# Attention's exponentials per head with a bias, and a later Square in the weight conversion

## The chip, the cores and the metric
One core of one Trainium2 chip runs the whole program in one launch. Its engines work side by side, each through its own queue in order: TensorE (PE for matmuls, PEld for the weight loads that go ahead of them), VectorE (DVE), ScalarE (ACT), GpSimd (POOL), and SyncE (SP), which only issues DMA transfers. The metric is the device time in microseconds (us) of one execution. Before the change it is 1010.89 us, the median of three runs (1010.03 to 1013.91).

## The reference
Three layers follow each other.

```python
k_p, v_p = mean of k, v over groups of 8 positions       # (4, 8, 72, 64)
scores = q @ k_p.T / 8                                   # (4, 8, 576, 72)
attn = exp(scores - max(scores)); attn /= attn.sum() + 1e-9
x = (attn @ v_p) as (2304, 512)
logits = x @ w_gate + log1p(exp(x @ w_noise)) * noise    # 8 experts
top2 = the two largest; weights = softmax over these two
out[token] = sum over its two experts e of weight * relu(x @ w1[e]) @ w2[e]
h = out @ w_in; g = max(0.01 * h, h); result = g @ w_out # 512 -> 2048 -> 512
```

All is float32, apart from `w_in` and `w_out`, which arrive as 64-bit floats and are narrowed to 32 bits on the chip.

## The kernel before
**Attention** goes over 18 tiles of 128 tokens. For one tile, `scores` multiplies the queries with the pooled keys of all 8 heads into one PSUM tile `qk` of two banks (8 heads of 72 columns, 576 in all). DVE reduces it to the maximum of each token and head (`mx`, 128x8, L364) and then subtracts that from all 576 columns into an SBUF tile `sm` (L366). `exponents` runs one exp over the 576 columns on ACT, with the scale 1/64 inside (L372). `transposed_exponents` transposes the result on PE in two halves of three (L380), and ACT copies each half out of PSUM (`at`, L381). `weighted` multiplies with the pooled values into another PSUM tile `av` (L388), ACT drains it (`avs`, L403), and `normalized` divides: DVE forms the reciprocal `rc` (L407, L408), POOL multiplies (L410, L413). `qk` and `av` take turns in three PSUM buffers.

The loop is skewed. In the turn of tile t, PE is given `scores(t+2)`, `transposed_exponents(t+1)` and `weighted(t)` in this order; its order is as written in the code. Those of DVE, ACT and POOL are made by a planner at compile time. Between these steps DVE also works on the router (`route`, with `work(budget)`), sums the keys of the next batch (`setup_keys`, L306) and splits the first expert weights (`split_half`, L156); POOL sums the values of the next batch (L324 to L326).

**The experts.** Each of 8 experts has up to 640 tokens. Float32 products are made of three matmuls on a high and a low part. For each expert, 8 calls of `hidden` (L742) are followed by 5 calls of `expert_out` (L763), each with a `transposed` (L215, L217, L218), which brings in a tile of the next expert's tokens. In `hidden`, ACT applies relu into the high part (L751), and DVE forms the low part (L752); the PSUM tile `ph` has two buffers. In `expert_out`, ACT copies the result out (`ys`, L773), and that PSUM tile has two buffers too. `feed` loads weights and splits them into two parts (ACT L154, DVE L156).

**The conversion** of the 64-bit weights is spread over the experts by calls of `narrow`. A call does a stage each for different pieces of 256 columns, of which there are 64: (1) for the 32 pieces of `w_in`, in pairs, a high and a low part of a converted tile (ACT L670, DVE L672); (2) the second half of the conversion of the last piece, a comparison and a product on DVE (L689), and sums on POOL (L700); (3) the first half of the conversion of another piece: four integer and float operations on DVE (L708, L711, L714, L715), then a sum on POOL (L718) and a Square on ACT (L719), which writes over a word that L715 has read; the comparison L689 of the next call reads it; (4) the load of a new piece. In this part of the kernel the orders of DVE and ACT are as written in the code, so what stands behind a waiting instruction waits too. PE's order here is the planner's.

A piece that is loaded in one call is first worked on two calls later, so 64 pieces need 69 calls until the last high and low parts are written. They are given so: 4 in the first expert's second pass of `hidden` and 3 behind it, 9 for each of the experts 1 to 6 (4 in `hidden`, at f = 0, 2, 4, 6, and 5 in `expert_out`), and 8 in the `hidden` of expert 7. That is 69.

**The last layer** (from 620 us on) gathers each token's two expert results and runs 512 to 2048 to 512 with the converted weights. The change leaves its code as it is.

Of the kernel before, what the change touches and what calls it, by code (L numbers as in the profile page):

```python
# [10 lines left out]
F32 = mybir.dt.float32  # L11
# [4 lines left out]
AF = mybir.ActivationFunctionType  # L16
ALU = mybir.AluOpType
# [4 lines left out]
P = 128  # L22
B, H, S, D = 4, 8, 576, 64
POOL = 8
J = S // POOL
# [3 lines left out]
E = 8  # L29
# [27 lines left out]
FH, FK, NF = 2, 2, 2  # L57
# [34 lines left out]
def pieces(t):  # L92
    got, n, end = [], t * P, (t + 1) * P
    while n < end:
        b = n // S
        m = min(end, (b + 1) * S) - n
        got.append((b, n - b * S, n - t * P, m))
        n += m
    return got
# [3 lines left out]
def body(ctx: ExitStack, tc, qT, kT, v, wgc, noise, eye, cst, w1, w2, win, wout, out):  # L103
    nc = tc.nc
# [53 lines left out]
    def feed(n, upto, pool=False):  # L158

        while loading:  # L160
            split_half(pool)
        for _ in range(n):
            if state["next"] < 2 * min(len(chunks), upto):
                c, h = divmod(state["next"], 2)
                state["next"] += 1
                raw = rawp.tile([P, 512], F32, tag="raw", name="raw")
                nc.sync.dma_start(raw, chunks[c][:, h * 512 : (h + 1) * 512])
                loading.append((c, h, raw))
# [33 lines left out]
    def gather(e, k):  # L202
        xg[e, k] = st.tile([P, DM], F32, tag="st", name="xg")
        i = k * E + e
        nc.gpsimd.indirect_dma_start(
            out=xg[e, k],
            out_offset=None,
            in_=x_d[0 : T1 * P if k < K1 else N, :],
            in_offset=bass.IndirectOffsetOnAxis(ap=gidx[:, i : i + 1], axis=0),
        )  # L210

    def transposed(src, dst, k):
        pt = b1.tile([P, 4, P], F32, tag="b1", name="xtp")
        for d in range(4):
            nc.tensor.transpose(pt[:, d, :], src[:, d * P : (d + 1) * P], ident)  # L215
        sl = slice(k * P, (k + 1) * P)
        nc.scalar.activation(dst[:, :, 0, sl], pt, AF.Copy)  # L217
        nc.vector.tensor_tensor(  # L218
            dst[:, :, 1, sl], pt, dst[:, :, 0, sl].bitcast(F32), op=ALU.subtract
        )  # L220

    with ExitStack() as actx:
        big = actx.enter_context(tc.tile_pool(name="qkav", bufs=3, space=PSUM))
        wk = actx.enter_context(tc.tile_pool(name="attw", bufs=2))
# [124 lines left out]
        sm, ex, at = {}, {}, {}  # L349

        def scores(t):
            ps = big.tile([P, 2, 512], F32, tag="big", name="qk")
            for b, s0, m0, m in pieces(t):
                for pr in range(4):
                    nc.tensor.matmul(
                        ps[m0 : m0 + m, pr // 2, (pr % 2) * 144 : (pr % 2) * 144 + 144],
                        qt[b][:, pr, s0 : s0 + m],
                        KB[b][:, pr, :],
                        start=True,
                        stop=True,  # L360
                    )
            view = ps[:, :, 0:288].rearrange("p a (h j) -> p a h j", j=J)
            mx = wk.tile([P, 2, 4], F32, tag="mx", name="mx")
            nc.vector.tensor_reduce(mx, view, axis=AX.X, op=ALU.max)  # L364
            sm[t] = wk.tile([P, 2, 4, J], F32, tag="sm", name="sm")
            nc.vector.tensor_tensor(  # L366
                sm[t], view, mx.unsqueeze(3).to_broadcast([P, 2, 4, J]), op=ALU.subtract
            )

        def exponents(t):  # L370
            ex[t] = sm[t].rearrange("p a h j -> p (a h j)")
            nc.scalar.activation(ex[t], ex[t], AF.Exp, scale=1.0 / 64.0)  # L372

        def transposed_exponents(t):
            at[t] = wk.tile([96, 6, P], F32, tag="at", name="at")
# [238 lines left out]
        for t in range(-2, T):  # L614
            if t + 2 < T:
                scores(t + 2)
# [11 lines left out]
            if t + 2 < T:  # L628
                exponents(t + 2)
# [32 lines left out]
    loaded, converting, parted = [], [], []  # L662

    def narrow():

        if parted and parted[0][1] is not None:
            i, part, w8, x = parted[0]
            sl = slice(512 * x, 512 * x + 512)
            hi = cv.tile([P, 512], F32R, tag="hi", name="cvhi", bufs=1)
            nc.scalar.activation(hi, w8[:, sl], AF.Copy)  # L670
            nc.sync.dma_start(combos[i][:, part, 0, sl], hi.bitcast(F32))
            nc.vector.tensor_tensor(  # L672
                w8[:, sl].bitcast(F32R), w8[:, sl], hi.bitcast(F32), op=ALU.subtract
            )
            nc.sync.dma_start(combos[i][:, part, 1, sl], w8[:, sl])
            parted[0][3] += 1
            if x:
                parted.pop(0)
        if converting:
            c, part, k, mf = converting.pop(0)  # L680
            if c < 8:
                w = cv.tile([P, CV], F32, tag="w", name="cvw")
            else:
                if part % 2 == 0:
                    w8 = cv.tile([P, 1024], F32, tag="cvq", name="cvq")
                    parted.append([c - 8, None, w8, 0])
                w8 = parted[-1][2]
                w = w8[:, part % 2 * CV : (part % 2 + 1) * CV]
            nc.vector.scalar_tensor_tensor(w, k, SMALL, mf, op0=ALU.is_ge, op1=ALU.mult)  # L689
            if c < 8:  # L690
                nc.sync.dma_start(singles[c][:, part * CV : (part + 1) * CV], w)
            elif part % 2:
                q = lambda i: w8[:, i * P : (i + 1) * P]
                for d, x, y, op in (
                    (S1, A21, A22, ALU.add),
                    (S2, S1, A11, ALU.subtract),
                    (S3, A11, A21, ALU.subtract),
                    (S4, A12, S2, ALU.subtract),
                ):
                    nc.gpsimd.tensor_tensor(q(d), q(x), q(y), op=op)  # L700
                parted[-1][1] = part // 2
        if len(loaded) > 1 or loaded and state["narrowed"] == 16 * 1024 // CV:
            c, part, raw = loaded.pop(0)
            low, high = raw[:, :, 0], raw[:, :, 1]
            a = cv.tile([P, CV], I32, tag="a", name="cva", bufs=1)
            m = cv.tile([P, CV], I32, tag="m", name="cvm")
            mf, hf, k = m.bitcast(F32), high.bitcast(F32), low.bitcast(F32)
            nc.vector.tensor_scalar(  # L708
                a, high, 3, 0x3FFFFFF8, op0=ALU.logical_shift_left, op1=ALU.bitwise_and
            )  # L710
            nc.vector.scalar_tensor_tensor(  # L711
                a, high, -0x40000000, a, op0=ALU.bitwise_and, op1=ALU.bitwise_or
            )
            nc.vector.tensor_single_scalar(m, a, -0x800000, op=ALU.bitwise_and)  # L714
            nc.vector.scalar_tensor_tensor(  # L715
                mf, low.bitcast(U32), 2.0**-52, mf, op0=ALU.mult, op1=ALU.mult
            )
            nc.gpsimd.tensor_tensor(mf, mf, a.bitcast(F32), op=ALU.add)  # L718
            nc.scalar.activation(k, hf, AF.Square)  # L719
            converting.append((c, part, k, mf))  # L720
        i = state["narrowed"]
        if i < 16 * 1024 // CV:
            state["narrowed"] += 1
            c, part = divmod(i, 1024 // CV)
            raw = cv.tile([P, CV, 2], I32, tag="raw64", name="raw64", bufs=3)
            words = doubles[c].bitcast(I32).rearrange("p (n t) -> p n t", t=2)
            nc.sync.dma_start(raw, words[:, part * CV : (part + 1) * CV])
            loaded.append((c, part, raw))
# [48 lines left out]
    def expert_out(e, k):  # L777
        for _ in expert_parts(e, k):
            pass
# [144 lines left out]
    with tc.manual_schedule(engines=ORDERED0):  # L924
# [12 lines left out]
        for k in range(K1):  # L937
            for i, _ in enumerate(expert_parts(0, k)):
# [4 lines left out]
                if k == K1 - 1 and i >= TI and late:  # L943
                    gather_late()
                    e, j = late.pop(0)
# [17 lines left out]
    with tc.manual_schedule(engines=ORDERED):  # L963
        for k in range(NB):
            transposed(xg[1, k], xT, k)
        for k in range(K1, NB):
            expert_out(0, k)
            feed(FK, 4 + RING)
            narrow()
        for e in range(1, E):  # L970
            for f in range(8):
                hidden(e, f)
                feed(FH, 8 * e + (f + 1) // 2 + RING)
                if f % NF == 0 or e + 1 == E:
                    narrow()
                next(tokens, None)
                if f >= 3 and e + 1 < E:
                    gather(e + 1, f - 3)
            if e + 1 == E:
                break  # L980
            for k in range(NB):
                transposed(xg[e + 1, k], xT, k)
                expert_out(e, k)
                feed(FK, 8 * e + 4 + RING)
                narrow()
# [30 lines left out]
    with tc.If(nover > 0):  # L1016
        with tc.tile_pool(name="over", bufs=1) as op:
# [30 lines left out]
            with tc.For_i(0, nover, 1) as j:  # L1048
# [13 lines left out]
                    op=ALU.mult,  # L1062
# [315 lines left out]
```

## Time and profile before

| | us |
|---|---|
| median of three runs | 1010.89 |
| all three | 1013.91, 1010.03, 1010.89 |
| the profiled execution | 1014.06 |
| its span, from the first to the last instruction | 1012.3 |
| PE busy in the span | 960.9 |
| DVE busy | 645.4 |
| ACT busy | 376.1 |

The profiled execution takes 1.8 us more than its span, and 3.2 us more than the median. The mean granted clock of TensorE is 0.979 of full speed. In the profile, a line like `L719` is a line of the kernel, `out<-in` are the program's names of the tiles, and a wait is put down to what released the waiting engine last. Attention is the time to about 113 us, the experts go on to about 610 us.

### The profile page before, as it was taken

How to read it: one execution, taken by the hardware profiler on the slowest of the kernel's cores; microseconds unless marked ns; L12 is line 12 of the kernel's file. 1: busy time of each engine (PE TensorE's matmuls, PEld its weight loads, DVE VectorE, ACT ScalarE, POOL GpSimd, SP SyncE). 2: the span in 40 equal slices, each digit the busy share in tenths (PEclk: the TensorE clock that was granted, in tenths of full speed). 3: DMA queues.
4: the chain of work that ended last, by engine and by line, in shares of the span. 5: the costliest groups of instructions: out<-in, count | busy, mean ns of one | idle time of the engine just before them, and what ended most of it. 6: DMA issues, size and time to landing. Idle time of an engine off the chain costs nothing. (4 is left out here: it accounts for less than half of the span.)

```text
span 1012.3 us, 15783 instructions
## 1 busy us (share of the span) xinstructions
PE 960.9 (95%) x5782; PEld 862.7 (85%) x5782; DVE 645.4 (64%) x1354; ACT 376.1 (37%) x729; POOL 228.2 (23%) x325
## 2 busy tenths in 40 slices
PE   6889879999999999999999998999999999999998
PEld 4788768998989899797897977989989988998897
DVE  5688855686775657766767833475566566556553
ACT  2644424443443434345353443332242232324112
POOL 2873452203122131422313222101001100000000
PEclk7889879999999999999999999999999999999999
DMA  9941346656465564866667586765646645645541
GB/s 267 323 156 62 101 143 194 219 175 210 147 192 164 187 185 157 264 202 222 213 207 224 201 285 229 257 247 207 230 171 210 244 168 200 222 148 193 213 146 42
DMA packets 85906, 198.09 MB, mean 196 GB/s; under 512 B 8960, under 2 KB 14528, under 8 KB 84672
## 3 DMA queue, kind: packets, MB, share of 16 engines
q1 hardware_dynamic: 79744, 177.11, 51.9%
q0 software_dynamic: 6080, 19.93, 6.5%
q8 instruction: 46, 0.75, 0.3%
q14 instruction: 36, 0.29, 0.1%
HBM read 156.11 MB, written 40.89 MB: 195 GB/s over the span
## 5 line engine op out<-in xcount | busy, mean ns | idle before, releaser
L1280 PE MATMUL po<-whB,gT 128*128 128x512 f32 x864 | 203.9, 392 | 0.0
L1280 PEld LDWEIGHTS po<-whB,gT 128*128 128x128 f32 x864 | 159.8, 188 | 31.9
L1244 PEld LDWEIGHTS pp<-zB,whA 128*128 128x128 f32 x1344 | 165.4, 192 | 6.9 <-ACT tmp L1252 3.5
L1244 PE MATMUL pp<-zB,whA 128*128 128x256 f32 x1344 | 167.7, 283 | 3.1 <-ACT tmp L1252 2.7
L763 PE MATMUL py<-whB,hT 128*128 128x512 f32 x600 | 148.8, 395 | 2.5 <-ACT ys L773 2.1
L742 PE MATMUL ph<-xT,whB 128*128 128x320 f32 x960 | 146.9, 309 | 2.4 <-ACT xT L217 2.4
L742 PEld LDWEIGHTS ph<-xT,whB 128*128 128x128 f32 x960 | 143.1, 188 | 5.8 <-ACT xT L217 3.1
L763 PEld LDWEIGHTS py<-whB,hT 128*128 128x128 f32 x600 | 109.6, 188 | 24.7 <-ACT ys L773 3.6
L1225 DVE TENSOR_TENSOR tmp<-tmp,pp 128x256 f32<-128x256 f32 x160 | 65.2, 418 | 65.5 <-PE pp L1244 61.6
L752 DVE SCALAR_TENSOR_TENSOR hT<-ph,hT 128x640 fp32r<-128x640 f32 (+2 forms) x72 | 53.9, 749 | 77.2 <-ACT hT L751 77.1
L742 PE MATMUL ph<-xT,whA 128*128 128x320 f32 (+2 forms) x576 | 94.2, 322 | 6.3 <-DVE hT L752 3.8
L742 PEld LDWEIGHTS ph<-xT,whA 128*128 128x128 f32 x576 | 90.2, 200 | 9.2 <-DVE hT L752 4.0
L763 PE MATMUL py<-whA,hT 128*128 128x512 f32 x360 | 89.3, 395 | 3.7 <-ACT ys L773 2.7
L1233 ACT ACTIVATE gT<-tmp 128x512 fp32r<-128x512 f32 x64 | 40.5, 632 | 134.5 <-DVE tmp L1230 134.5
L719 ACT ACTIVATE raw<-raw 128x256 f32<-128x256 f32 x64 | 28.1, 438 | 163.9 <-DVE cvm L715 132.7
L895 POOL DMA_INDIRECT g<-y_d,rows x36 | 34.0, 945 | 242.3 <-DVE g L906 167.8
L763 PEld LDWEIGHTS py<-whA,hT 128*128 128x128 f32 x360 | 65.6, 188 | 18.8 <-ACT ys L773 4.3
L718 POOL TENSOR_TENSOR cvm<-cvm,cva 128x256 f32<-128x256 f32 x64 | 48.0, 750 | 138.0 <-DVE cvm L715 120.8
L1234 DVE TENSOR_TENSOR gT<-tmp,gT 128x512 fp32r<-128x512 f32 x64 | 44.3, 692 | 46.3 <-ACT gT L1233 46.3
L751 ACT ACTIVATE hT<-ph 128x640 fp32r<-128x640 f32 (+2 forms) x72 | 45.9, 638 | 64.6 <-PE ph L742 64.6
L156 DVE TENSOR_TENSOR whB<-raw,whB 128x512 fp32r<-128x512 f32 x89 | 58.7, 688 | 10.5 <-ACT whB L154 10.3
L154 ACT ACTIVATE whB<-raw 128x512 fp32r<-128x512 f32 x96 | 57.2, 624 | 12.7 <-DMA raw<-in_w 8.3
(192 smaller groups left out, 1144.8 us busy)
## 6 DMA issues: line engine op xcount, KB each, us to landing
whA<-ws SPq DMA_DIRECT2D x64, 896.0 KB
raw<-in_w SPq DMA_DIRECT2D x128, 256.0 KB
y_d<-ys SPq DMA_DIRECT2D x40, 256.0 KB
raw<-in_wout SPq DMA_DIRECT2D x32, 256.0 KB
raw<-in_win SPq DMA_DIRECT2D x32, 256.0 KB
ws<-cvhi SPq DMA_DIRECT2D x32, 256.0 KB
ws<-cvq SPq DMA_DIRECT2D x32, 256.0 KB
whA<-ws SPq DMA_DIRECT2D x10, 512.0 KB
```

The source lines that it names most:

```text
L154: nc.scalar.activation(s[:, 0, sl], raw, AF.Copy)
L156: eng.tensor_tensor(s[:, 1, sl], raw, s[:, 0, sl].bitcast(F32), op=ALU.subtract)
L718: nc.gpsimd.tensor_tensor(mf, mf, a.bitcast(F32), op=ALU.add)
L742: nc.tensor.matmul(ps[:, h, 0:m], w[:, a, col : col + P], xT[:, d, b, m0:m1], start=(d == 0 and a == 0 and b == 0), stop=(d == 3 and a == 1),)
L751: nc.scalar.activation(hv[:, 0], src, AF.Relu)
L752: nc.vector.scalar_tensor_tensor(hv[:, 1], src, 0.0, hv[:, 0].bitcast(F32), op0=ALU.max, op1=ALU.subtract)
L763: nc.tensor.matmul(ps, hT[:, f, a, sl], w[:, b, col : col + DM], start=(f == 0 and a == 0 and b == 0), stop=(f == 7 and a == 1),)
L1225: add = lambda o, x, y: nc.vector.tensor_tensor(o, x, y, op=ALU.add)
L1233: nc.scalar.activation(gT[:, h, 0], ch(h), AF.Copy)
L1234: nc.vector.tensor_tensor(gT[:, h, 1], ch(h), gT[:, h, 0].bitcast(F32), op=ALU.subtract)
L1244: nc.tensor.matmul(out_, w[:, part, a, q * P : (q + 1) * P], zT["B"][:, j, part, b], start=(part == 0 and a == 0 and b == 0), stop=(part = ...
L1280: nc.tensor.matmul(sums[t], gT[:, h, a, sl], w[:, b, h * DM : (h + 1) * DM], start=(fp + h + a + b == 0), stop=(fp == 7 and h == 1 and a = ...
```

## The change
Three edits. In attention, the subtraction L366 goes. The maximum is multiplied by -1/64 into a small tile `shift` (128x8), and the exp reads the scores from PSUM, head by head, with the head's column of `shift` as its bias: 8 activations of 72 columns in place of one of 576. In `narrow`, the Square of a piece moves from the first half of its conversion to the beginning of the second half, one call later. And the calls of `narrow` in `hidden` stand at f = 0, 2, 4, 5, 6 for the experts 1 to 6 and at f = 0, 2, 4, 6 for expert 7.

```diff
             nc.vector.tensor_reduce(mx, view, axis=AX.X, op=ALU.max)
-            sm[t] = wk.tile([P, 2, 4, J], F32, tag="sm", name="sm")
-            nc.vector.tensor_tensor(
-                sm[t], view, mx.unsqueeze(3).to_broadcast([P, 2, 4, J]), op=ALU.subtract
-            )
+            shift = wk.tile([P, 2, 4], F32, tag="shift", name="shift")
+            nc.vector.tensor_scalar_mul(shift, mx, -1.0 / 64.0)
+            sm[t] = view, shift
 
         def exponents(t):
-            ex[t] = sm[t].rearrange("p a h j -> p (a h j)")
-            nc.scalar.activation(ex[t], ex[t], AF.Exp, scale=1.0 / 64.0)
+            view, shift = sm.pop(t)
+            e = wk.tile([P, 2, 4, J], F32, tag="sm", name="sm")
+            for a in range(2):
+                for h in range(4):
+                    nc.scalar.activation(
+                        e[:, a, h],
+                        view[:, a, h],
+                        AF.Exp,
+                        bias=shift[:, a, h : h + 1],
+                        scale=1.0 / 64.0,
+                    )
+            ex[t] = e.rearrange("p a h j -> p (a h j)")
...
         if converting:
-            c, part, k, mf = converting.pop(0)
+            c, part, k, hf, mf = converting.pop(0)
+            nc.scalar.activation(k, hf, AF.Square)
...
             nc.gpsimd.tensor_tensor(mf, mf, a.bitcast(F32), op=ALU.add)
-            nc.scalar.activation(k, hf, AF.Square)
-            converting.append((c, part, k, mf))
+            converting.append((c, part, k, hf, mf))
...
-                if f % NF == 0 or e + 1 == E:
+                if f % 2 == 0 or f == 5 and e + 1 < E:
                     narrow()
```

## Rows read from the trace of the kernel before
**Rows 1.** The page's first part: each engine's busy time, share of the span, instructions.
```profile
PE 960.9 (95%) x5782; PEld 862.7 (85%) x5782; DVE 645.4 (64%) x1354; ACT 376.1 (37%) x729; POOL 228.2 (23%) x325
```
**Rows 2.** Busy time by stage: stretch, length, each engine, granted clock, DMA share, GB/s.
```profile
25.00:113.00 88.00, 76.70 (x556) 71.05 (x554) 71.53 (x205) 44.81 (x88) 54.80 (x91) 0.90 0.52 166
...
156.00:398.00 242.00, 241.04 (x1382) 220.33 (x1383) 162.25 (x362) 99.22 (x188) 50.99 (x61) 1.00 0.57 180
398.00:600.00 202.00, 191.62 (x1063) 169.11 (x1062) 143.93 (x273) 90.48 (x173) 59.74 (x98) 1.00 0.67 221
```
**Rows 3.** PE's waits, 156 to 600: who for whom, us in total, times, longest.
```profile
PE py L763 <- ACT ys L773: 4.8, 6, 1.6
PE ph L742 <- ACT xT L217: 3.7, 3, 1.4
PE py L763 <- ACT hT L751: 1.4, 3, 0.5
```
**Rows 4.** ACT's longest wait, 156 to 600 us.
```profile
ACT raw L719 <- DVE cvm L715: 132.7, 48, 3.4
```
**Rows 5.** Timeline around 411 us: start, us, engine, line, tiles, count, idle before.
```profile
408.65 0.68 DVE L672 TENSOR_TENSOR cvq<-cvq,cvhi 128x512 fp32r<-128x512 f32 x1
...
411.00 0.64 DVE L715 SCALAR_TENSOR_TENSOR cvm<-raw,cvm 128x256 f32<-128x256 uint32 x1
411.67 0.44 ACT L719 ACTIVATE raw<-raw 128x256 f32<-128x256 f32 x1 [3.13 <-DVE cvm L715]
...
412.48 0.58 ACT L773 ACTIVATE ys<-py 128x512 f32<-128x512 f32 x1
...
413.12 4.18 PEld L763 LDWEIGHTS py<-whA,hT 128*128 128x128 f32 x19 [1.06 <-ACT ys L773]
```
**Rows 6.** DVE's longest wait, 156 to 600 us.
```profile
DVE hT L752 <- ACT hT L751: 75.1, 54, 5.0
```
**Rows 7.** Timeline of one turn of hidden in expert 7.
```profile
571.65 0.82 DVE L752 SCALAR_TENSOR_TENSOR hT<-ph,hT 128x640 fp32r<-128x640 f32 x1 [1.10 <-ACT hT L751]
...
572.39 1.28 DVE L156 TENSOR_TENSOR whB<-raw,whB 128x512 fp32r<-128x512 f32 x2
...
573.04 3.68 PE L742 MATMUL ph<-xT,whB 128*128 128x320 f32 x24
```
**Rows 8.** PE's longest wait in attention, 25 to 113 us.
```profile
PE atp L380 <- ACT sm L372: 6.6, 4, 3.6
```
**Rows 9.** Timeline of one attention tile, from its maximum to its transposes.
```profile
76.31 0.86 ACT L381 ACTIVATE at<-atp 96x384 f32<-96x384 f32 x2 [1.84 <-PE atp L380]
...
76.81 0.75 DVE L364 TENSOR_REDUCE mx<-qk 128x8 f32<-128x576 f32 x1
...
78.39 0.68 ACT L372 ACTIVATE sm<-sm 128x576 f32<-128x576 f32 x1 [1.21 <-DVE sm L366]
...
79.29 0.82 PE L380 MATMUL atp<-ident,sm 128*96 128x128 f32 x6
```
**Rows 10.** ACT's groups by shape: xcount, busy us, mean ns, idle before and its releasers.
```profile
L670 ACT ACTIVATE cvhi<-cvq 128x512 fp32r<-128x512 f32 x32 | 20.0, 625 | 1.6 <-DMA ws<-cvhi 1.5
L381 ACT ACTIVATE at<-atp 96x384 f32<-96x384 f32 x36 | 16.3, 483 | 15.7 <-PE atp L380 15.5
L905 ACT ACTIVATE g<-g,gates 128x512 f32<-128x512 f32 x18 | 12.8, 714 | 3.9 <-DMA g<-y_d,rows 3.9
L403 ACT ACTIVATE avs<-av 128x648 f32<-128x648 f32 x18 | 12.7, 705 | 11.0 <-PE av L388 7.5 <-PE counts L582 1.3 <-PE vtp L332 1.1
```
**Rows 11.** One line's instructions: ns min/median/max, first and last start, form.
```profile
L407 DVE TENSOR_SCALAR rc<-avs x18: 158/172/1046, 27.5 to 114.0; 128x8 f32<-128x8 f32 x18
```
**Rows 12.** Timeline of the longest wait for an exponential.
```profile
58.65 3.83 DVE L156 TENSOR_TENSOR whA<-raw,whA 128x512 fp32r<-128x512 f32 x2
...
63.98 0.31 PE L380 MATMUL atp<-ident,sm 128*96 128x128 f32 x1 [3.62 <-ACT sm L372]
```
**Rows 13.** Busy time, columns as in Rows 2, behind that wait.
```profile
64.00:70.00 6.00, 6.00 (x31) 5.91 (x32) 3.92 (x15) 3.65 (x8) 2.21 (x7) 0.60 0.33 116
```

## The prediction
> **What bounds the kernel now.** I read the page's busy line first: PE is busy for 95% of the span, no other engine for more than 64% [rows 1]. So time can only be won where PE is idle or runs at the lower clock, and it is lost where another engine starts to hold PE. The table of busy time by stage says where that is [rows 2]. From 156 to 398 us PE is idle for 242 - 241.0 = 1.0 us, from 398 to 600 us, where the heavier pieces of `w_in` are converted, for 202 - 191.6 = 10.4 us. In attention, from 25 to 113 us, it is idle for 11.3 us of 88, and the granted clock is 0.90 there, 1.00 in the other two. These three stretches are what the change touches. Before 25 us and after 600 us I leave everything as it is.
>
> PE's waits from 156 to 600 us name ACT: the copy of a result (L773), the copy of a new tile (L217), and a relu (L751), together 9.9 of the 11.4 us [rows 3]. ACT is busy for less than half of this time [rows 2], so I asked what ACT waits for. The Square stands in the way for 132.7 us, 48 times [rows 4]. The timeline around 411 us shows how this reaches PE: ACT stands for 3.13 us before the Square, until DVE has finished L715; the copies behind it run as soon as it is done; PE has then stood for 1.06 us for the second of them [rows 5].
>
> In attention, PE's longest wait is for the exponential: 6.6 us in four waits, one of them 3.6 us [rows 8].
>
> **The Square, one call later.** Nothing is added or removed: still 64 Squares of 0.44 us [rows 5]. At its new place what it needs was finished in the call before, so ACT no longer stops there. The new wait is DVE's: L689 now needs a Square of the same call, and behind L689 stand the four conversion operations and the next low part L752, on which a PSUM buffer of PE hangs. What hides the Square is the DVE operation ahead of L689: L672 with 0.68 us, the split L156 with 1.28 us for two, or L752 with 0.82 us [rows 5, 7], each released by the ACT instruction just ahead of the Square and each longer than 0.44 us. Without that cover it costs DVE 64 x 0.44 = 28 us, out of 138 us that DVE is idle from 156 to 600 us [rows 2]. DVE should even gain: it waits 75.1 us for the relu [rows 6], some of which stands behind a blocked Square (1.10 us in one turn [rows 7]).
>
> What is late next where PE's waits go? The same copies, now bound by ACT's own queue: about six instructions of 0.4 to 0.7 us in a call against PE's 3.7 us [rows 7] for a turn of `hidden` and about 6 us for one of `expert_out`. Some waits will stay, for a transpose behind L218 for instance. Of 11.4 us of idle time I take 9 as won; the bounds are 0, if DVE turns out to be what holds PE, and 11.4.
>
> **The calls at f = 5.** Six calls are added (experts 1 to 6) and four go (expert 7). With 71 calls against 69 needed, the last call that does something is the second one of expert 7. The work is the same, but expert 7, in whose `hidden` every turn had a call, is freed early, which belongs to the 9 us above. The price is a run of three turns with calls, f = 4, 5, 6. A heavy call takes DVE from 408.65 to 411.64, or 3.0 us [rows 5]; with L752 in each turn and two splits in the even ones [rows 7] that is 3 x 3.0 + 3 x 0.82 + 2 x 1.28 = 14.0 us against 3 x 3.68 = 11.0 us of PE. DVE falls back by 3 us and catches up in the turn f = 7, which has no call. PE has a second PSUM buffer, worth one turn of 3.68 us, so I count it as nothing; if that cover is short by 1 us, it costs 6 us over six experts. The loads and stores of these calls go through SP's queue as before, a turn earlier.
>
> **Attention: DVE and ACT.** On DVE, the subtraction goes; between the end of `mx` (77.56) and the end of the exponential (79.07) it and the exponential take 1.51 us [rows 9]. The shift comes in. The nearest operation is L407, the same 128x8 in SBUF: 158 ns at least, 172 in the median, up to 1046 [rows 11]. I take 0.35 us, near the median, with something for the stretched ones; both ends stay in the range.
>
> On ACT, one instruction of 0.68 us becomes eight of 72 columns, of a kind that the trace doesn't have. Two PSUM reads give the slope: (705 - 483) / (648 - 384) = 0.84 ns for a column, so 72 columns without a pointer take 483 - 312 x 0.84 = 221 ns [rows 10]. The pointer: L905, with one as its scale, takes 714 ns, L670 of the same 128x512 without it 625 [rows 10], so 0.09 us more. One head alone takes 0.31 us. They should overlap: two of 0.483 us fill only 0.86 us [rows 9], 0.11 us less than their sum. So 8 x (0.31 - 0.11) + 0.11 = 1.7 us; the bounds are 1.0 us (the pointer hidden) and 2.5 us (no overlap). I take 1.7.
>
> The Trainium skill, in "ScalarE: Activation LUTs", section "What ACT_TABLE_LOAD costs", speaks against this edit: an ACTIVATE with immediates costs 186 ns and 0.833 ns per column, each pointer 93 ns on top, and neighbours overlap by 93 ns. By that, as an estimate, 8 x 0.246 + 0.09 = 2.1 us, and the late tiles below would cost 3 us more in sum. Slope and pointer agree with the rows named above; fixed cost and overlap come out a little worse than there.
>
> So from the end of `mx` to the last exponential it takes 0.35 + 0.1 (handing over) + 1.7 = 2.15 us in place of 1.51: 0.65 us later (bounds: 0.25 us earlier, 2.1 us later). In total ACT gets some 18 us more and DVE some 7 us less, against 44.8 and 71.5 us busy of 88 [rows 2]; neither is full, so what counts is lateness. The exponential waits nowhere new for its PSUM tile: `av` takes the buffer of the scores whose transposes PE has just done, and these need the exponentials anyway.
>
> In 8 of the 18 tiles, counted in the timeline, the exponential ends less than 0.6 us before the transposes start; one is shown, with 79.07 to 79.29 [rows 9]. Four of these are PE's waits [rows 8], and there 0.65 us is lost in full, 2.6 us; in the other four what exceeds the margin, 1.3 us in sum. The other ten have 1.5 us or more. Against that stands DVE's relief: 0.4 us less per tile ahead of the next maximum. I take 1.5 us for it. Attention: 2.6 + 1.3 - 1.5 = +2.4 us.
>
> **The sum.** 1014.06 (profiled execution) - 9 + 2.4 = 1007.5 us. This execution was 3.2 us over the median of 1010.89, so in terms of the median 1004.3 us; its own range is 1000 to 1008.
>
> **Rivals.**
> *More is won (994 us).* At 58.65 us DVE put two splits (3.83 us) between a maximum and its subtraction, and PE stood for 3.62 us [rows 12]; behind that the granted clock was 0.60 for 6 us [rows 13], which costs 6 x 0.4 = 2.4 us. If the planner puts the shift right behind the maximum, the exponential can run during the splits. All four waits [rows 8] and that clock: 6.6 + 2.4 = 9.0 us less, and nothing of the 2.4 us lost: 1010.9 - 9 - 9 + 1 = 994. For it: the shift is short. Against: something stood between the two in most tiles, and the shift depends on the maximum as the subtraction did.
>
> *No change (1010 us).* DVE, not ACT, holds PE in the conversion. From 398 to 600 us it is busy for 143.9 of 202 us [rows 2], the calls become denser, and its order is fixed. Then ACT's freedom only moves the wait on to DVE: 3 us won, 2.4 lost, 1010.3. For it: DVE waits on ACT and ACT on DVE by turns [rows 4, 6], so taking one wait can feed the other. Against: PE's waits name ACT's copies, which need nothing of DVE.
>
> *Slower (1023 us).* ACT's eight instructions don't overlap (2.5 us) and POOL stretches the shift (1.05 us): 2.1 us later in the 8 tight tiles, 16 us in all, and two more falls of the clock [rows 13], 5 us: 1010.9 - 9 + 21 = 1023. It decides from 9 us lost in attention on, about 1.3 us per tight tile; from 14 us, or 2 us per tile, it is over 0.5% slower. For it: POOL is busy for 55 of these 88 us [rows 2], and the 1046 ns have occurred [rows 11]. Against: the median there is 0.17, and two neighbours do overlap [rows 9].
>
> **Chances.** The forecast 0.45, more won 0.13, no change 0.25, slower 0.17. About 0.5%, or 5 us, is what a measurement of this kernel can tell from no change. Of the forecast's cases 0.7 lie below 1005.8, all of the second, few of the third: faster 0.45. Within 0.5%: 0.14 from the forecast, most of the third, a little of the fourth, 0.39. Slower 0.16. The range from 996 to 1014 leaves out part of the second case and most of the fourth.
>
> **What would show it.** Square: ACT's wait on L715 gone, and PE's idle time from 156 to 600 us down from 11.4 to 2 or 3 us. If DVE's wait for the Square at L689 appears with over 10 us, the cover is wrong. Calls: PE's wait for L752 near f = 7. Attention: eight activations in 1.7 us, the shift at 0.2 to 0.4 us, PE's wait for the exponentials at 9 us rather than 6.6. Wrong would be a clock below 0.85 from 25 to 113 us, or a PE idle time there of over 20 us.

## The result and the profile after

The changed kernel takes 998.7 us (median; 997.5 to 1002.6) against 1011.5 us: the ratio is 0.9878, with a 95% interval from 0.9844 to 0.9912. Measured a second time (e10 below) it was 0.9913, 0.9879 to 0.9947. So it is faster by about 1%, where 1004.3 us, or 0.65%, had been forecast. The profiled execution takes 998.06 us, its span is 996.2 us.

The page's busy line and the stages, against [rows 1, 2] (the new lines of code shift the numbers: L719 is now L690, L752 is L761, L773 is L782, L742 is L751, L763 is L772, L380 is L389, L372 is L374):

```profile
PE 952.0 (96%) x5782; PEld 857.8 (86%) x5782; DVE 637.4 (64%) x1354; ACT 393.7 (40%) x855; POOL 230.5 (23%) x325
```
```profile
25.00:113.00 88.00, 76.77 (x568) 70.42 (x568) 64.81 (x205) 60.47 (x200) 56.29 (x91) 0.94 0.50 168
...
156.00:398.00 242.00, 240.47 (x1385) 219.89 (x1384) 176.29 (x389) 102.60 (x196) 57.15 (x72) 1.00 0.62 192
398.00:600.00 202.00, 199.92 (x1119) 179.06 (x1118) 132.88 (x250) 90.69 (x169) 57.80 (x91) 1.00 0.70 231
```

From 398 to 600 us PE's idle time fell from 10.4 to 2.1 us (3.9 in e10, the same kernel). In attention it is 11.2 us as before (11.3), although DVE is busy for 7 us less and ACT for 16 us more. The waits of the three engines from 156 to 600 us, PE first, then ACT, then DVE, answer to [rows 3, 4, 6]:

```profile
PE py L772 <- ACT ys L782: 1.4, 3, 0.5
PE ph L1191 <- ACT early L217: 0.7, 1, 0.7
PE ph L751 <- ACT xT L217: 0.6, 1, 0.6
PE ph L751 <- DVE xT L218: 0.5, 1, 0.5
```
```profile
ACT hT L760 <- PE ph L751: 136.3, 62, 3.7
ACT ys L782 <- PE py L772: 42.2, 18, 4.5
ACT cvhi L679 <- DMA ws<-cvhi: 18.7, 12, 3.1
```
```profile
DVE hT L761 <- ACT hT L760: 59.1, 36, 3.3
...
DVE cvq L699 <- ACT raw L690: 5.3, 2, 3.2
DVE cvw L699 <- ACT raw L690: 4.5, 2, 3.0
```

The reader is to see the direction turn round. ACT waited for DVE, and PE for ACT; now ACT waits for PE, which is the engine that sets the time. The timeline of the same place as [rows 5] shows why: the Square (L690) runs right behind the high part (L679), the copies L217 and L782 follow at once, and only then does DVE get to L699 and its four operations.

```profile
405.36 0.62 ACT L679 ACTIVATE cvhi<-cvq 128x512 fp32r<-128x512 f32 x1
...
405.88 0.43 ACT L690 ACTIVATE raw<-raw 128x256 f32<-128x256 f32 x1
406.18 0.69 DVE L681 TENSOR_TENSOR cvq<-cvq,cvhi 128x512 fp32r<-128x512 f32 x1
406.21 0.58 ACT L217 ACTIVATE xT<-xtp 128x512 fp32r<-128x512 f32 x1
406.68 0.59 ACT L782 ACTIVATE ys<-py 128x512 f32<-128x512 f32 x1
406.79 0.42 DVE L699 SCALAR_TENSOR_TENSOR cvq<-raw,cvm 128x256 f32<-128x256 f32 x1
...
408.54 0.63 DVE L725 SCALAR_TENSOR_TENSOR cvm<-raw,cvm 128x256 f32<-128x256 uint32 x1
```

PE's longest waits in attention (25 to 113 us) and one tile of its timeline, against [rows 8, 9]:

```profile
PE atp L389 <- ACT sm L374: 3.4, 2, 1.8
PE pidx L562 <- ACT vT L333: 2.9, 1, 2.9
PE av L397 <- ACT avs L412: 2.4, 1, 2.4
PE qk L355 <- ACT sm L374: 1.9, 1, 1.9
```
```profile
74.02 0.70 DVE L364 TENSOR_REDUCE mx<-qk 128x8 f32<-128x576 f32 x1
...
74.61 1.05 POOL L422 TENSOR_TENSOR xt<-avs,rc 128x512 f32<-128x512 f32 x1
74.76 0.93 DVE L366 TENSOR_SCALAR shift<-mx 128x8 f32<-128x8 f32 x1
...
75.73 1.80 ACT L374 ACTIVATE sm<-qk,shift 128x72 f32<-128x72 f32 x8 [1.34 <-DVE shift L366]
76.31 1.58 PE L389 MATMUL atp<-ident,sm 128*96 128x128 f32 x6
```

The waits now name ACT almost alone. In the tile shown the shift took 0.93 us, all of it beside a POOL instruction, and the eight exponentials 1.80; the transposes began 0.58 us after the first exponential, since the first of them need only the first heads, and took 1.58 us in place of 0.82, waiting for the others within. Such a wait is counted as PE's busy time.

To compare stages over the runs, I took from each timeline the start of ACT's copies of results (L773 before) in three stretches: from the second copy (the first expert's second) to the twentieth (end of expert 3, with what is left of the first expert), to the thirty-fifth (end of expert 6), and to the fortieth (end of expert 7). From the last on, the rest takes 399.6 us before and after. Each row is a single execution; the kernels e1 to e12 come further down.

| profiled execution | 2nd copy at | to the end of expert 3 | 4 to 6 | 7 | 2nd to 40th |
|---|---|---|---|---|---|
| before | 155.2 | 211.5 | 183.6 | 62.5 | 457.6 |
| after | 152.3 | 211.8 | 174.9 | 57.6 | 444.4 |
| e1, attention only | 152.4 | 211.4 | 184.6 | 61.4 | 457.4 |
| e2, Square and calls | 155.9 | 211.5 | 176.2 | 57.6 | 445.3 |
| e3, Square only | 151.0 | 211.1 | 174.2 | 61.2 | 446.5 |
| e4, calls only | 149.7 | 212.2 | 195.5 | 57.9 | 465.6 |
| e5, all but the calls | 164.7 | 211.3 | 174.1 | 59.3 | 444.7 |
| e8, Square with its own tile | 154.8 | 210.8 | 174.1 | 60.2 | 445.2 |
| e12, Square twice | 149.6 | 210.9 | 174.2 | 59.5 | 444.7 |
| e9, e3 with eight exponentials | 159.9 | 211.4 | 174.8 | 64.5 | 450.7 |
| e10, the changed kernel again | 152.0 | 211.9 | 176.6 | 57.6 | 446.2 |
| e11, the changed kernel without the shift | 151.0 | 211.6 | 176.4 | 57.6 | 445.6 |

So of the 16.0 us between the two profiles, 13.2 lie between the second and the last copy, none of them in experts 1 to 3, and 2.9 in the first 155 us. In the second profile of the changed kernel (e10) the 13.2 are 11.4: these stages vary by 2 us between executions of one kernel, and expert 7 by more (59.3 to 64.5 us with one and the same order of instructions in e3, e5 and e9).

### The profile page after: what moved, and what is told of

The parts are those of the page before. It is cut to its first block, busy times and chain, and to the rows that moved or that the text cites. A ratio compares the mean times of both kernels' runs of the same rounds, so it can differ in the third digit from the quotient of the medians.

```text
span 996.2 us, 15949 instructions
## 1 busy us (share of the span) xinstructions
PE 952.0 (96%) x5782; PEld 857.8 (86%) x5782; DVE 637.4 (64%) x1354; ACT 393.7 (40%) x855; POOL 230.5 (23%) x325
## 5 line engine op out<-in xcount | busy, mean ns | idle before, releaser
L772 PE MATMUL py<-whB,hT 128*128 128x512 f32 x600 | 147.3, 395 | 0.5 <-ACT ys L782 0.5
L751 PE MATMUL ph<-xT,whB 128*128 128x320 f32 x960 | 146.4, 309 | 0.6 <-ACT xT L217 0.6
L751 PEld LDWEIGHTS ph<-xT,whB 128*128 128x128 f32 x960 | 143.1, 188 | 3.1 <-ACT xT L217 0.8
L772 PEld LDWEIGHTS py<-whB,hT 128*128 128x128 f32 x600 | 110.4, 189 | 22.5 <-ACT ys L782 1.7
L751 PE MATMUL ph<-xT,whA 128*128 128x320 f32 (+2 forms) x576 | 91.0, 314 | 5.2 <-DVE hT L761 3.6
L751 PEld LDWEIGHTS ph<-xT,whA 128*128 128x128 f32 x576 | 86.9, 191 | 8.2 <-DVE hT L761 4.2
L761 DVE SCALAR_TENSOR_TENSOR hT<-ph,hT 128x640 fp32r<-128x640 f32 (+2 forms) x72 | 53.5, 746 | 59.4 <-ACT hT L760 59.1
L772 PE MATMUL py<-whA,hT 128*128 128x512 f32 x360 | 87.4, 394 | 0.9 <-ACT ys L782 0.9
L772 PEld LDWEIGHTS py<-whA,hT 128*128 128x128 f32 x360 | 66.3, 188 | 14.8 <-ACT ys L782 2.0
L156 DVE TENSOR_TENSOR whB<-raw,whB 128x512 fp32r<-128x512 f32 x89 | 59.8, 707 | 11.2 <-ACT whB L154 11.2
L205 POOL DMA_INDIRECT xg<-x_d,gidx x40 | 40.4, 1011 | 70.2 <-PE xtp L215 57.1
```

The lines of the kernel that those rows point to most:

```text
L156: eng.tensor_tensor(s[:, 1, sl], raw, s[:, 0, sl].bitcast(F32), op=ALU.subtract)
L751: nc.tensor.matmul(ps[:, h, 0:m], w[:, a, col : col + P], xT[:, d, b, m0:m1], start=(d == 0 and a == 0 and b == 0), stop=(d == 3 and a == 1),)
L761: nc.vector.scalar_tensor_tensor(hv[:, 1], src, 0.0, hv[:, 0].bitcast(F32), op0=ALU.max, op1=ALU.subtract)
L772: nc.tensor.matmul(ps, hT[:, f, a, sl], w[:, b, col : col + DM], start=(f == 0 and a == 0 and b == 0), stop=(f == 7 and a == 1),)
```

## The experiments

All ratios are against the kernel before, measured beside them on the same chip, with 95% intervals. e1 to e4, e5 to e8 and e9 to e12 ran on a chip each, so between these groups the ratios are the better comparison.

**e1: the new attention alone.** The diff is the attention part of the change and nothing else.

> Before, with the new attention alone (eight exponentials per tile from PSUM, no subtraction). If ACT's blocked queue in the experts made the gain, this gives little: attention itself unchanged (its end at 112 to 114 us) and at most the 2.9 us that the stretch from 113 to 155 us was shorter after the change, so a time 0 to 4 us under before, ratio 0.996 to 1.000. Rival, the relief of VectorE in attention is worth more than the profile of the whole change shows: 5 us or more, ratio under 0.995. Second rival, the stretch from 113 to 155 us was shorter by chance: ratio 1.000 and a granted clock near 0.84 there.

Measured: 1.0019 (0.9987 to 1.0051). ACT's wait before the Square is all there in its trace:

```profile
ACT raw L728 <- DVE cvm L724: 129.9, 47, 3.4
```

By itself the new attention is no gain, perhaps a small loss, in spite of its 152.4 us for the first stretch.

**e2: the later Square and the calls, old attention.** The diff is the rest of the change.

> Before, with the later Square and the new places of the calls, attention as it was. If the gain of the experts (13.2 us between 155 us and the last copy of a result in the profiles) is theirs alone, the time falls by 10 to 13 us, ratio 0.987 to 0.990, and PE is idle for 1 to 3 us instead of 11.4 from 156 to 600 us. Rival, attention's new order brought part of it: ratio 0.992 or more.

Measured: 0.9891 (0.9859 to 0.9922). The gain is theirs, and with 445.3 us it lies between the second and the last copy as expected.

**e3: the later Square alone.**

```diff
-            c, part, k, mf = converting.pop(0)
+            c, part, k, hf, mf = converting.pop(0)
+            nc.scalar.activation(k, hf, AF.Square)
...
-            nc.scalar.activation(k, hf, AF.Square)
-            converting.append((c, part, k, mf))
+            converting.append((c, part, k, hf, mf))
```

> Before, with the later Square alone; calls and attention as they were. If ScalarE standing before the Square is what held TensorE, this gives most of the gain: ScalarE's wait on L715 (132.7 us) gone, PE idle from 156 to 600 us down from 11.4 to 2 to 4 us, time 8 to 11 us under before, ratio 0.989 to 0.992; what is left lies in expert 7, where every turn of hidden has a call. Rival, VectorE's load in the dense turns holds TensorE: 3 us or less, ratio 0.997 or more, and TensorE's waits move to VectorE (L752, L218).

Measured: 0.987 (0.9839 to 0.99), 998.6 us: this one move gives the whole gain. Of PE's waits of [rows 3] from 156 to 600 us, the first two are left, with 1.8 us in place of 8.5; the longest wait is now another, on DVE:

```profile
PE xtp L215 <- DVE g L906: 2.7, 1, 2.7
PE py L763 <- ACT ys L773: 1.5, 2, 1.0
...
PE ph L742 <- ACT xT L217: 0.3, 1, 0.3
```

That one stands at the end of expert 7, where PE wants the first gathered tile of the last layer. All profiles with the old calls and a free Square have it, with 1.4 to 3.6 us; those with the new calls don't.

**e4: the calls alone.**

```diff
-                if f % NF == 0 or e + 1 == E:
+                if f % 2 == 0 or f == 5 and e + 1 < E:
```

> Before, with the new places of the calls alone; the Square stays where it blocks ScalarE. If the blocked queue is the cause, the two extra calls per expert in a row only add blocks: expert 7 gains 4 to 5 us (stretch from 550 to 613 us), the experts 1 to 6 lose 0 to 3 us, time 1 to 5 us under before, ratio 0.995 to 0.999. Rival, the density of the calls is the cause: 8 us or more, ratio under 0.992.

Measured: 1.0053 (1.003 to 1.0076), so slower. Expert 7 did gain 4.6 us (62.5 to 57.9), but the experts 4 to 6 lost 11.9 (183.6 to 195.5). There are still 64 Squares; what the calls at f = 5 change is that blocked ones follow each other in three turns. PE's waits for ACT grew in all three of [rows 3]:

```profile
PE py L763 <- ACT ys L773: 5.9, 9, 1.5
PE py L763 <- ACT hT L751: 5.5, 3, 3.2
PE ph L742 <- ACT xT L217: 5.1, 3, 2.6
```

In the trace, the ACT instructions behind 14.5 of these 16.5 us ran without a gap after a Square that had waited for DVE; before, it is 7.4 of the 9.9 us. I had expected a small gain; the loss per call was worse than I took. Both theories on record were wrong about the sign.

**e5: all but the calls.** The diff to the changed kernel is e4's, reversed.

> The changed kernel with the calls back at f = 0, 2, 4, 6 and at every turn of expert 7: the later Square and the new attention are left. The later Square alone gave 0.987, the new attention alone 1.002. If the three parts add up, this gives 0.986 to 0.990, and expert 7 (from the last copy of expert 6 to that of expert 7) takes 60 to 62 us, against 57.6 with the new calls. Rival: the calls are needed to turn the freed ScalarE into time; then 0.991 or more.

Measured: 0.9917 (0.9887 to 0.9947), 1002.2 us: by its value just inside what the rival said, by its interval in both. Expert 7 took 59.3 us, a little under the 60 to 62 that were expected. From the second copy to the last it takes 444.7 us, no more than with the calls (444.4), so the calls are not needed. But its profiled execution, with 1010.8 us the slowest of its twelve, came to the second copy only at 164.7 us, against 152.0 in e10's and 152.3 in the first profile of the changed kernel. Up to the second pass over the first expert the three have the same order of instructions on PE, DVE and ACT. The attention stage of e5, then of e10:

```profile
25.00:113.00 88.00, 74.72 (x498) 67.47 (x497) 54.57 (x162) 54.13 (x177) 51.30 (x85) 0.83 0.50 158
```
```profile
25.00:113.00 88.00, 75.77 (x570) 69.32 (x569) 63.24 (x206) 60.54 (x201) 56.49 (x91) 0.95 0.50 167
```

PE was busy about as long in both, but with a granted clock of 0.83 it did 498 matmuls in place of 570. So the first 155 us jump by 12 us from one execution to another, with the same instructions in the same order. Why the clock was lower there stays open.

**e6: no shift, old calls.** The keys are scaled by -1/64 as they are copied, and the minimum is taken; it is then itself the bias. The diff is against e5.

```diff
-                nc.scalar.activation(KB[b][half, :, i * J : (i + 1) * J], kp[half], AF.Copy)
+                nc.scalar.activation(
+                    KB[b][half, :, i * J : (i + 1) * J], kp[half], AF.Copy, scale=-1.0 / 64.0
+                )
...
-            nc.vector.tensor_reduce(mx, view, axis=AX.X, op=ALU.max)
-            shift = wk.tile([P, 2, 4], F32, tag="shift", name="shift")
-            nc.vector.tensor_scalar_mul(shift, mx, -1.0 / 64.0)
-            sm[t] = view, shift
+            nc.vector.tensor_reduce(mx, view, axis=AX.X, op=ALU.min)
+            sm[t] = view, mx
...
-                        scale=1.0 / 64.0,
+                        scale=-1.0,
```

> As e5_no_calls, but the keys are scaled by -1/64 as they are copied, the minimum is taken in place of the maximum, and it is itself the bias: VectorE's shift (L366, 0.2 us in the median) is gone, ScalarE's eight instructions are as before. If the lateness of the exponentials behind the maximum costs time in attention, up to 0.3 us in some 8 tiles come back: 1 to 4 us under e5_no_calls, attention ends 1 to 3 us earlier. Rival: attention's length is set by something else (the router on VectorE, the clock): no difference from e5_no_calls beyond 3 us.

Measured: 0.985 (0.9804 to 0.9896), 995.6 us, 6.6 under e5; more than expected, though the two intervals just overlap.

**e7: one exponential without the maximum, old calls.** The kernel still takes the maximum but leaves out its subtraction. The diff is against e5.

```diff
-            shift = wk.tile([P, 2, 4], F32, tag="shift", name="shift")
-            nc.vector.tensor_scalar_mul(shift, mx, -1.0 / 64.0)
-            sm[t] = view, shift
+            sm[t] = view
...
-            for a in range(2):
-                for h in range(4):
...
+            nc.scalar.activation(e, sm.pop(t), AF.Exp, scale=1.0 / 64.0)
```

> As e5_no_calls, but with one exponential of 576 columns per tile from PSUM, without the maximum (which is still taken, but not subtracted, so the part of the computation that guards against overflow is left out). VectorE is relieved of 0.75 us per tile as in the change and ScalarE keeps its single instruction of 0.7 us. If VectorE's relief is worth something and ScalarE's eight instructions ate it, this is 4 to 10 us under e5_no_calls and PE's wait for the exponentials in attention falls under 1 us. If neither matters (the router's chain and the clock set attention's length), it is within 3 us of e5_no_calls.

Measured: 0.986 (0.9817 to 0.9904), 995.1 us. That is 7.1 us under e5, as the first theory had it, but only 3.5 under e3 with the old attention. The intervals separate it from neither.

**e8: the Square at its old place with a tile of its own.**

```diff
-            mf, hf, k = m.bitcast(F32), high.bitcast(F32), low.bitcast(F32)
+            mf, hf = m.bitcast(F32), high.bitcast(F32)
...
+            k = cv.tile([P, CV], BF16, tag="sq", name="sq")
             nc.scalar.activation(k, hf, AF.Square)
```

> Before, with the Square at its old place in ScalarE's order, but writing into a small tile of its own (in 16 bits, for want of room) in place of the word that L715 reads: so it waits for the load only, not for VectorE. Attention and calls as before. If the wait of ScalarE for L715 is the cause, this gives the same as the later Square alone: ratio 0.985 to 0.990, and PE idle for 5 us or less from 156 to 600 us. Rival: the later place, or the planner's other order of TensorE that came with it, made the gain; then 0.995 or more.

Measured: 0.9881 (0.9843 to 0.992). The Square stands where it stood and no longer waits for DVE:

```profile
L720 ACT ACTIVATE sq<-raw x64: 412/422/441, 172.4 to 565.8; 128x256 bf16<-128x256 f32 x64
...
  ACT ys L774: 0.4, 1
```

(ns min/median/max, then all of the idle time ahead of it, in us.) So the gain doesn't need the later place: it comes when ACT no longer waits for L715. The rival that names the planner's order of PE is not settled by this: PE's order in the experts differs from before in e8 as it does in e3.

**e9: eight exponentials, but with the subtraction kept, old calls.** ACT's part of the edit without DVE's, on top of e3.

```diff
-            ex[t] = sm[t].rearrange("p a h j -> p (a h j)")
-            nc.scalar.activation(ex[t], ex[t], AF.Exp, scale=1.0 / 64.0)
+            e = sm[t]
+            for a in range(2):
+                for h in range(4):
+                    nc.scalar.activation(e[:, a, h], e[:, a, h], AF.Exp, scale=1.0 / 64.0)
+            ex[t] = e.rearrange("p a h j -> p (a h j)")
```

> The later Square with the old calls, and attention with the subtraction kept and eight exponentials of 72 columns each from SBUF without a bias: ScalarE's lateness alone, without VectorE's relief. e3_square_only (old attention) had 0.987, e7_one_exponential (relief alone) 0.986. If the eight instructions cost what the prediction took, 0.4 to 0.65 us in some 8 tiles and nothing against it, this is 2 to 5 us over e3: 0.989 to 0.992. Rival: lateness of this size is lost in what the clock does to the first 155 us: within 2 us of e3, 0.985 to 0.989.

Measured: 0.9963 (0.9934 to 0.9992), 1008.9 us: 10 us over e3, and 9 over e12 on the same chip, about twice the upper expectation. One head takes 250 ns here, from SBUF and without a pointer:

```profile
L374 ACT ACTIVATE sm<-sm 128x72 f32<-128x72 f32 x144 | 24.2, 250 | 15.9 <-DVE sm L366 14.0 <-DVE y L456 1.9
```

Eight of them fill 1.33 us in its timeline, 0.65 us more than the single one. How much of the 10 us is this lateness and how much the planner's other order of DVE and ACT was not separated. Nor is all of it attention's: between the second and the last copy, where the order is e3's, its profile took 450.7 us against 446.5.

**e10: the changed kernel again.**

> The changed kernel once more, for a direct comparison on this chip with the next one: 0.986 to 0.990 as before. If the changed attention makes the first 155 us jump more than the old one did, some runs lie over 1005 us.

Measured: 0.9913 (0.9879 to 0.9947), 1001.5 us, with executions from 998.4 to 1013.2.

**e11: the changed kernel without the shift.** The diff is e6's, with the calls of the change.

> The changed kernel without the shift: keys scaled by -1/64, the minimum itself the bias. If e6_no_shift (995.6 us) against e5_no_calls (1002.2 us) was the shift's worth, this is 3 to 7 us under e10_changed_again. If the difference there came from the clock in the first 155 us, it is within 2 us of it.

Measured: 0.9828 (0.9793 to 0.9863), 994.8 us, 6.7 under e10 on the same chip, with intervals that don't meet. It has the lowest median of all, though e6 and e7 are not separated from it. The shift is not the only difference: the planner, which makes the orders of DVE, ACT and POOL in attention, made others here, in dozens of places on DVE alone. PE waits for the exponentials hardly at all (25 to 113 us); what holds it there is the work on the values:

```profile
PE atp L389 <- DVE VB L346: 5.7, 2, 4.1
PE vtp L334 <- POOL vp L328: 2.9, 2, 1.5
...
PE atp L389 <- ACT sm L374: 0.3, 1, 0.3
```

**e12: every Square twice, otherwise as e3.**

```diff
             nc.scalar.activation(k, hf, AF.Square)
+            nc.scalar.activation(k, hf, AF.Square)
```

> e3_square_only with every Square done twice in a row, so ScalarE has 64 x 0.43 = 28 us more between 156 and 590 us. If the Square lies hidden behind VectorE's L672, L156 or L752 and ScalarE has room, the time stays within 2 us of e3's 998.6 and VectorE's waits for the Square at L691 stay under 15 us in all. If ScalarE's queue is tight, the copies that TensorE waits for come later: 4 us or more over e3.

Measured: 0.9888 (0.985 to 0.9925), 999.8 us against e3's 998.6, with 444.7 us between second and last copy. DVE's waits for either Square (the second is L682) are 9.3 us in all, 8.8 of them in these two rows:

```profile
DVE cvw L691 <- ACT raw L682: 6.6, 6, 3.2
...
DVE cvw L691 <- ACT raw L681: 2.2, 1, 2.2
```

## Why the prediction was right, and where its sizes were off

**The cause.** That PE waited for ACT's copies, and these for a Square that waited for DVE, was right. Two edits that free the Square in different ways, by the later place (e3) and by another tile to write to (e8), give the same 11 to 12 us between the second and the last copy; blocked Squares in more turns running (e4) make it worse. In the trace before, 7.4 of the 9.9 us that PE waited for ACT were for a copy or relu that ran without a gap behind a blocked Square, as in [rows 5]. What no run separates is the planner's share: wherever the Square is free (e3, e8, e12 and the change), PE's order in the experts is another than before too.

**The size of that term.** I took 9 us; it was 13.2 in the first profile of the changed kernel and 11.4 in e10. The error is in the bound: I had put the most that can be won at PE's idle time, 11.4 us from 156 to 600 us. From the second to the last copy, before and after:

```profile
155.15:612.73 457.58, 444.58 (x2499) 398.26 (x2496) 309.06 (x638) 193.47 (x368) 116.14 (x165) 1.00 0.63 203
```
```profile
152.26:596.65 444.39, 441.15 (x2498) 399.45 (x2496) 309.54 (x638) 193.89 (x368) 116.58 (x165) 1.00 0.65 209
```

Idle time fell by 9.8 us, as forecast, but busy time fell too, by 3.4 us for the same matmuls (444.6 to 441.2; 440.9 to 441.3 in all other profiles with a free Square but e9's, with 443.2 and a clock of 0.97 in expert 7). A wait also hides in what counts as PE's busy time, though the planner's other order may have a share in these 3.4 us. The weight loads show more of the waits; their waits for ACT in these stretches, before and after:

```profile
PEld py L763 <- ACT ys L773: 7.9, 8, 2.0
PEld ph L742 <- ACT xT L217: 4.8, 4, 1.9
PEld py L763 <- ACT hT L751: 3.1, 4, 0.9
```
```profile
PEld py L772 <- ACT ys L782: 3.7, 7, 0.9
...
PEld ph L751 <- ACT xT L217: 1.1, 2, 0.8
```

That is 15.8 us against 4.8. The prediction itself mixed the two up in one place: the 1.06 us of [rows 5] are the weight load's wait, the matmuls beside it had 0.64.

```profile
413.12 3.24 PE L763 MATMUL py<-whA,hT 128*128 128x512 f32 x13 [0.64 <-ACT ys L773]
```

The forecast's own range of 1000 to 1008 us was missed by the first measurement (998.7) and met by the second (1001.5); both lie in the stated 996 to 1014. PE's idle time from 156 to 600 us came down to 3.6 us (5.4 in e10), where I had named 2 or 3.

**The calls at f = 5.** That expert 7 is freed early was half right: it became 2 to 4 us shorter by the calls (59.3 to 61.2 in e3, e5, e8 and e12, 57.6 in e2), and PE's wait for the last layer's first tile at its end, 1.4 to 2.7 us in these four, is gone with them. But the experts 4 to 6 gave back about as much (174.2 in e3; 176.2 in e2, and 174.9 and 176.6 in the two profiles of the changed kernel), and from the second to the last copy the change itself, e10, e2 and e5 lie within 2 us of each other. "I count it as nothing" holds with the later Square only; with the old one (e4) the three calls in a row cost the experts 4 to 6 12 us, 8 us net of what expert 7 gained.

**The cover of the Square.** It held: DVE waits for it 9.8 us, in four places, just under the 10 us that I had named. Doubling it cost nothing that these intervals can tell. What I missed is what is late next. It is not a copy in ACT's own queue: the high part L679 now waits 18.7 us for the store of its only buffer, 12 times up to 3.1 us, and stands in ACT's queue as the Square did. PE loses little by it.

**Attention.** I took +2.4 us. e1 says +1.9 (-1.3 to +5.2), e10 against e2 +2.2, e5 against e3 +4.7, the first measurement of the changed kernel against e2 -1.3: the sum fits, but it is not measured to better than some 3 us. Its parts probably don't fit. I took 3.9 us for the late exponentials and 1.5 for DVE's relief. In e9, eight exponentials with the subtraction kept cost 9 to 10 us; from there to the new attention (e5) 5 to 7 come back. If these are the two terms, both were too small by two to four times and the sum fits by luck, as their errors cancel; but the planner's orders change along with each step, so this is not shown. One exponential came out at 337 ns in the median (I had 310), eight of them at 1.80 us (1.7). By (8 x 0.337 - 1.80) / 7, neighbours overlapped by 0.13 us. The Trainium skill ("ScalarE: Activation LUTs", "What ACT_TABLE_LOAD costs") gives 186 + 60 + 93 = 339 ns for one, as an estimate, which agrees; by its overlap of 93 ns eight would take an estimated 2.1 us, and the measured 1.80 decides.

Two readings of the prediction were a little off without changing its sum: of the ten tiles that were said to have 1.5 us or more to spare, one has 0.60 us and one 1.44.

The shift is the step whose weight I may have missed most. I had it at 0.35 us per tile, and that was its mean (0.33, 6.0 us in all), but as a detail of the chain that counts in the tight tiles only. Without it the kernel is 6.7 us faster (e11 against e10) or 6.6 (e6 against e5), about as if every bit of it counted. Since the planner made other orders in those kernels, it is not shown that the shift's own time is the cause, and the two profiles don't show where the time went: their second copies come at 152.0 and 151.0 us. The trace gives the shift's sum and mean, and its spread:

```profile
L366 DVE TENSOR_SCALAR shift<-mx 128x8 f32<-128x8 f32 x18 | 6.0, 334 | 0.2
...
L366 DVE TENSOR_SCALAR shift<-mx x18: 110/209/929, 17.7 to 105.7; 128x8 f32<-128x8 f32 x18
```

Eight of the 18 had no POOL instruction beside them and took 110 to 171 ns; the ten that overlapped one took 164 to 929. So the stretching that the prediction feared did occur beside POOL, but over the 1.05 us of the slower case only once, in e10 (1.44).

Also wrong was that nothing new waits for the PSUM tile of the scores: PE waited 1.9 us to write new ones until the exponentials had read the old (`qk <- ACT sm` above).

**The rivals.** "No change, DVE holds PE" fell with e3. "More is won" did not come in the changed kernel: the four waits for exponentials became two of 3.4 us in all, and others took their place. e11 nearly reached its size (994). "Slower" fell with 1.80 us for eight. One sign that I had named as wrong did occur, a clock below 0.85 from 25 to 113 us, but only in e5's slowest execution (0.83); the two profiles of the changed kernel have 0.94 and 0.95.

**Open.** The 2.9 us that the first 155 us were shorter in the profiles are not shown to be the change's: with one order of instructions this stretch took from 149.6 to 155.9 us in the kernels with the old attention, and 152.0 to 164.7 with the new one. Of 28 executions with the new attention and the later Square (the change, e10, e5) eight took over 1004 us, of 24 with the old attention and a free Square (e2, e3, e8, e12) none. That speaks for the new attention making long ones more frequent. It is not shown to be the cause, since the kernel before has some executions 7 to 9 us over its median too.

## What to carry to other kernels
Look in an in-order queue for the instruction that waits on another engine ahead of work that the bottleneck needs, and give it its inputs a turn earlier or a tile of its own: ACT stood for 133 us before the Square, and one moved line (e3) won about 11 us. Take an idle engine's wait seriously by what stands behind it, and don't bound a gain by the idle time of a busy engine, since waits hide in its busy time; its weight loads show more of them. In a chain across engines, look at the small step that every turn has to pass (here a 128x8 multiplication): the kernel that folds it into a scale of a copy that is made anyway was 6.7 us faster, and that copy (L311) takes 438 ns with the scale and 440 without. When a planner makes the orders, an edit changes them too, and a difference in time belongs to both until a run separates them.

## What was not expected of the hardware
The first 155 us of one and the same order of instructions took 152.0 us in one execution and 164.7 in another, with a granted clock of 0.95 and 0.83 of full speed from 25 to 113 us. A DVE multiplication of 128x8 took 110 to 171 ns with no POOL instruction beside it, and up to 929 ns with one. Eight activations of 72 columns from PSUM, each with a pointer, overlapped by 0.13 us each, eight from SBUF without one by 0.1 (e9), two of 384 columns before by 0.11. PE's matmuls can count as busy while their weight loads wait: in [rows 5] the weight load stood for 1.06 us and the matmuls for 0.64.
